# A chunked state-space scan feeding a maxout network: masks and exponents of the second chunk moved three groups forward, a weight decode moved into the next block, and the opening's transposes reordered

## The chip, the cores and the metric

The kernel runs on one core of one Trainium2 chip. The metric is the device time of one execution in microseconds (us); a smaller number is better. The instruction times below come from one profiled execution; the times of whole runs come from executions of the same program.

## The reference, cut to what matters

A Mamba2-like scan over 768 positions runs for 4 batches and 8 heads, with head size 32 and state size 16. Its output is laid out as 3072 tokens by 256 and goes through a maxout network with three input matrices and one output matrix.

```python
cum = np.cumsum(log_a_chunk, axis=-1)
L = np.exp(cum[:, :, :, None] - cum[:, :, None, :]) * causal
CB = np.einsum('bhin,bhjn->bhij', Cc, Bc)
y = einsum('bhij,bhjd->bhid', CB * L, xc) + einsum('bhin,bhnd->bhid', Cc, state) * exp(cum)
state = exp(sum la) * state + sum_j Bc[j] xc[j] * exp(cum[-1] - cum[j])
...
h = np.maximum(np.maximum(x @ w1, x @ w2), x @ w3)     # 256 -> 768
out = h @ w_out                                        # 768 -> 256
```

## The kernel before, in words

The sequence is cut into 6 chunks of 128 positions, numbered 0 to 5 (called c; the text counts chunk 1 as the second). For each chunk the attention part makes the 256-wide rows of 512 tokens (4 batches by 128 positions), called yT, and the network part of that chunk follows while the attention of the next chunk is worked on between its matmuls. The order on every engine is the order of the program text; nothing is rescheduled. TensorE (PE) makes all products into PSUM, VectorE (DVE) and ScalarE (ACT) empty PSUM, GpSimd (POOL) works between SBUF tiles, and almost all transfers are issued by SyncE (SP) in one order. Each transfer of SP uses one of eight completion semaphores in turn, and waits before it starts until the transfer eight places earlier on that semaphore has landed.

The stages around the change, in order:

- *Opening, chunk 0.* The decay matrix L0 of chunk 0 is made for the four batches b by matmuls into PSUM (`spread_i`, L335), an exponent straight from PSUM for b = 0 and 1 (`first_exps`, L367, ACT) or first a sum on DVE (`first_sums`, L362) for b = 2 and 3. B and C are transposed on PE (`scan_b`, `scan_tc`, both L434) and copied out by ACT (`BT` L430, `CT` L449, two instructions). `first_scores` (L533) multiplies them on PE, `first_weights` (L542, DVE) multiplies the scores into L0, four head pairs r = 0 to 3 for each pair of batches, and `first_own` (L607) makes y. Beside this, the running sums of the logarithms of all other chunks are made: `logs` (L267, ACT), `running` (L272, DVE, tile a_sb); SP writes them to DRAM (L962, rows_dram), reorders them (L966, cums), and later reads them back spread over the partitions, as L (`decay_load`, L390) and as E (`last_load`, L397, eight transfers).
- *Block 0.* A loop over n = 0 to 17 makes the maxout products of chunk 0 (`up`, L655, four 128x512 passes for each n) and evicts them (L1072 on ACT for the first matrix, L1074 on DVE for the maximum). The weights arrive in a packed form, so in every second n one piece is decoded: two ACT instructions (L184, L193), two on DVE (L185, L188), one on POOL (L194), which is `decode`, and one on DVE one round later (L197), which is `sign`. There are twelve pieces: nine for the three input matrices, and three for the output matrix.
- *Chunk 1's attention inside block 0.* `decay_masks` (L405, POOL, two instructions for each pair of batches) masks L, at n = 6 and n = 8. `part` makes one eighth of the exponents of L (L415, ACT, four instructions of 128x64), each after the mask of its pair. At n = 11 B and C are transposed. At n = 12 ACT makes the exponent of E (`scan_e`, L453), DVE makes Cd = C transposed times E (`scan_cd`, L460) and the scores go into four PSUM banks. `scan_weight` (L560, DVE) multiplies each bank of scores into L for one r: three of them stand on DVE's queue right behind Cd. At n = 14 `scan_state` (L504, tile A) needs two PSUM banks: the first is the bank that Cd reads and the second is the bank that the weighting of r = 0 reads. `scan_own` (L595) makes y from the weighted L; `scan_old` (L578) adds the part of the old state.
- *Block 1 and later.* The products of the network use a seven-product scheme for 2x2 blocks (`early` and `late`, both L705, for k = 0 to 8), with sums of yT (`scan_sums`, L630, DVE, four instructions of which each second one needs the one before it) and of weights (`weight_sums`, L690 to L693, POOL). In `early` the order of products is 1, 6, 5, 7; product 5 needs the first of the four yT sums, product 6 the second, product 7 the third. `early` is emptied by one ACT copy (L730) and three DVE sums (L731 to L733). Twelve pieces of chunk 0's output product (`down_next`, L891, four passes each) are put between them by a written list (X1, where each D is one piece): 1 and 2 pieces stand ahead of block 1, then one at k = 0, two at k = 1 and so on. The fifth and sixth piece need the last decoded part of the output matrix.

The parts of chunk 1's exponents and the downs of block 1 are placed by these lines:

```python
        if n in (6, 8):
            decay_masks(1, n - 6)
...
        part(1, {8: 1, 9: 2, 11: 1, 12: 2, 13: 1, 14: 1}.get(n, 0))
...
    X1 = ["tc", "DD", "D", "s", "D", "AD", "y", "D", "DD"]
```

Of the kernel before, what the change touches and what calls it, by code (L numbers as in the profile page):

```python
# [19 lines left out]
def kernel(  # L20
# [25 lines left out]
    NB, NH, S, D = x.shape  # L46
# [4 lines left out]
    NP = NH // 2  # L51
# [160 lines left out]
    def sign():  # L212

        unsigned.pop(0)()
# [50 lines left out]
    def logs(src, name):  # L265
        lg = const.tile(list(src.shape), FP32, name=name)
        nc.scalar.activation(lg, src, AF.Ln)  # L267
        return lg

    def running(rows, lg, out, keep):  # L270
        for w in range(out.shape[1]):
            nc.vector.tensor_tensor_scan(  # L272
                out=out[:, w], data0=keep[0:rows], data1=lg[:, w], initial=0.0,
                op0=ALU.mult, op1=ALU.add)
# [89 lines left out]
    def first_exps(b, summed, gs=range(2)):  # L364
        for g in gs:
            part = L0[:, b, g * HALF:(g + 1) * HALF]
            nc.scalar.activation(part, part if summed else spread[b, g], AF.Exp)  # L367
# [70 lines left out]
    def scan_tc(c, kind):  # L438
        st = blocks[c]
        st["trC"] = tr = kind([HN, NB, P], "trC")  # L440
        transposes(tr, st["C"])

    def scan_c(c):

        st = blocks[c]
        tr = st["trC"]
        st["CT"] = CT = att.tile([HN, NB, 2, P], FP32, tag="CT", bufs=1, name="CT")
        for g in range(2):
            nc.scalar.mul(CT[:, :, g], tr, parity[:, g:g + 1])  # L449
# [14 lines left out]
    def scan_bd(c):  # L464
        st = blocks[c]
        st["Bd"] = Bd = att.tile([P, BH, N], FP32, tag="Bd", bufs=1, name="Bd")
        nc.gpsimd.tensor_tensor(
            out=Bd, in0=st["B"], in1=from_j[c].unsqueeze(2).to_broadcast([P, BH, N]),
            op=ALU.mult)
# [233 lines left out]
    def products(c, k, which, first):  # L703
        for p, bank, half in which:
            nc.tensor.matmul(  # L705
                out=bank[:, half], lhsT=left(p, k), rhs=sides[c][p],
                start=(first and half == 0), stop=True, skip_group_check=True)
# [10 lines left out]
    def early(c, k):  # L718
        q, i = divmod(k, 3)
        A, B = (sum_bank(kind, [P, 2, HB]) for kind in "AB")  # L720
        products(c, k, [(1, A, 0), (6, A, 1), (5, B, 0), (7, B, 1)], True)
        if i == 0:
            held["m"] = ffn.tile([P, 4, HB], FP32, tag="m", name="m")

        if i > 0 and k % 2 not in quarters:
            quarters[k % 2] = kilos(HB)[:, 0:3]
        t = held["m"][:, 1:4] if i == 0 else quarters[k % 2]
        eu = wtmp.tile([P, 2, HB], FP32, tag="w_u", name="eu")
        v = wtmp.tile([P, 2, HB], FP32, tag="w_r", name="v")[:, 0]
        nc.scalar.copy(out=eu[:, 0], in_=A[:, 0])  # L730
        nc.vector.tensor_tensor(out=eu[:, 1], in0=A[:, 1], in1=eu[:, 0], op=ALU.add)  # L731
        nc.vector.tensor_tensor(out=v, in0=B[:, 1], in1=eu[:, 1], op=ALU.add)  # L732
        nc.vector.tensor_tensor(out=t[:, 2], in0=B[:, 0], in1=v, op=ALU.add)  # L733
        held["open"] = A, B, eu, t
# [215 lines left out]
    scan_b(0, ffn_bank)  # L950
    first_sums(2)
    scan_bd(0)
    first_exps(1, False)
    spread_banks(3, (att_bank, att_bank))
    spread_i((3,), True)
    clip(a_sb)
    first_sums(3)
    scan_tc(0, ffn_bank)
    scan_c(0)
    lg = logs(a_sb, "lg")  # L960
    running(R, lg, a_sb, keep2)
    nc.sync.dma_start(  # L962
        out=rows_dram.rearrange("k c s -> (k c) s").rearrange("(w r) s -> r w s", w=2), in_=a_sb)
# [17 lines left out]
    decode()  # L981
    first_exps(2, True, (1,))
    first_exps(3, True, (1,))
    s01 = first_scores(0)
    s23 = first_scores(2, {r: ffn_bank([P, 2, 2, P], "s") for r in (2, 3)})
    state_sum = first_state(att_bank)
    ncums_tp = turned(R, a_sb, "ncums", ffn_bank)
    first_weights(0, s01)

    aside = ffn.tile([P, 4, HB], FP32, tag="m", name="m")  # L990
    for j, s in enumerate(s23.values()):
# [59 lines left out]
    for n in range(NF * 3):  # L1051
        j, g = divmod(n, 2)
        q, i = divmod(j, 3)
        f = 2 * q + g
        if n == 0:
            pair = [ffn_bank([P, BLK], "up") for _ in range(2)]
            group(pair[0], 0, 0, (0,))
            first_own((2, 3))
            group(pair[1], 0, 1, (0,))
            for p, ff in zip(pair, range(2)):  # L1060
                group(p, 0, ff, (1,))
        if j > 0:
            p = ffn_bank([P, BLK], "up")
            whole_group(p, i, f)
        else:
            p = pair[g]
        if i == 0 and g == 0:
            m = ffn.tile([P, 4, HB], FP32, tag="m", name="m")
        pop({13: 2, 14: 1, 15: 2, 16: 1}.get(n, 0))
        mg = m[:, 2 * g:2 * g + 2].rearrange("p r t -> p (r t)")  # L1070
        if i == 0:
            nc.scalar.copy(out=mg, in_=p)  # L1072
        else:
            nc.vector.tensor_tensor(  # L1074
                out=mg if i == 1 else h_of(0)[:, f], in0=mg, in1=p, op=ALU.max)
        if g == 0 and n <= 16:
            sign()
            decode()
        if n == 1:
            fj = from_last(R, a_sb, "fj", HP)  # L1080
        if n == 3:
            first_tokens()
            load(2, "B")
            fetch()
            load(2, "C")
            fetch()
            decay_load(2, (0,))
            last_load(2)
            home(2, "x")
        if n in (6, 8):  # L1090
            decay_masks(1, n - 6)
        if n == 11:
            transposed(1)
            scan_bd(1)
            scan_c(1)
        if n == 12:
            scan_e(1)
            scan_cd(1)
            scores(1)
        part(1, {8: 1, 9: 2, 11: 1, 12: 2, 13: 1, 14: 1}.get(n, 0))  # L1100
        if n == 14:
            later.extend(scan_state(1, att_bank))
        if n == 15:
            shared["att"] = False
            places()
            weight_sums(0)
        if n == 16:
            scan_own(1, (0, 1))
        if n == 17:
            weight_sums(1)  # L1110
# [8 lines left out]
    pop(9)  # L1119
    transposed(2, False)  # L1120
    scan_bd(2)
    decode()
    down_next()
    down_next()

    X1 = ["tc", "DD", "D", "s", "D", "AD", "y", "D", "DD"]
    Y1 = 9 * [""]  # L1130
    P1 = [(1, 0, 0), (1, 0, 0), (0, 0, 2), (1, 0, 1), (0, 1, 1), (1, 1, 2), (1, 0, 1), (1, 0, 1),
          (1, 0, 2)]
# [10 lines left out]
    for c in range(1, NC):  # L1143
        n = c + 1
        xs, ys, ps_, ds, ks = (
            (X1, Y1, P1, D1, K1) if c == 1 else (X2, Y2, P2, D2, K2) if n < NC else
            (X3, Y3, P3, D2, {}))
        for k in range(NW):
            if k == 0 and n == NC:
                pop(1)  # L1150
            early(c, k)
            if c == 1 and k == 0:
                sign()
            part(n, ds[k][0])
            part(n + 1, ds[k][1])
            pop(ps_[k][0])
            if k == 0 and c > 1:
                if n < NC:
                    scan_bd(n)
                hidden_sums(c - 1, nc.gpsimd, (0 if c < NC - 1 else NQ - 1, NQ))  # L1160
            if c >= NC - 2 and k in (3, 6):
                hidden_sums(c, nc.gpsimd, (k // 3 - 1, k // 3))
            x = xs[k]
            if n == NC:
                last_next(k)
            elif x in ("D", "DD"):
                for _ in x:
                    down_next()
            elif x == "AD":
                later.extend(scan_state(n, att_bank))  # L1170
                down_next()
            elif x == "tc":
                scan_tc(n, att_bank)
                down_next()
            elif x == "t":
                transposed(n)
            elif x == "s":
                scores(n)
            elif x == "y":
                scan_old(n)  # L1180
                scan_own(n)
                scan_y(n)
                scan_sums(n)
            pop(ps_[k][1])
            maximum = late(c, k)
            if c == 1 and k + 2 < NW:
                weight_sums(k + 2)
            if c == 1 and k == NW - 2:
                output_weight_sums()
            if n < NC and k == 0:  # L1190
                loads(c + 2)
            if n < NC and k == 0:
                scan_c(n)
            if n < NC and k == int(c == 1):
                scan_e(n)
                later.append(lambda: scan_cd(n))
            flush()
            pop(ps_[k][2])
            later[:0] = maximum
            if ys[k] == "D":  # L1200
                down_next()
                flush()
            if k in ks and n + ks[k][0] < NC:
                decay_masks(n + ks[k][0], ks[k][1])
        if n == NC:
            pop(9)
        add_downs(c)
# [31 lines left out]
```

## Time and profile before

| what | value |
|---|---|
| median of three runs | 295.79 us (292.7 to 296.08) |
| the profiled execution's own time | 292.7 us |
| its span from first to last instruction | 291.0 us |
| PE busy | 278.3 us, 96% of the span |
| DVE, POOL, ACT busy | 209.3, 123.4, 111.9 us |
| DMA queue of the data | 88476 packets, 22.39 MB, 42.3% of 16 engines |

The profiled execution is the fastest of the three runs and lies 3.1 us under their median. A line of the timeline has the start and the duration in us, engine, line, operation, tiles, shape, count, and in brackets how long the engine was idle before it and what released it. SPq is SyncE issuing a transfer: its duration is that of the issue, not of the transfer. PE times of matmuls are pipelined, so a busy PE is not necessarily at its peak.

### The profile page before, as it was taken

How to read it: one execution, taken by the hardware profiler on the slowest of the kernel's cores; microseconds unless marked ns; L12 is line 12 of the kernel's file. 1: busy time of each engine (PE TensorE's matmuls, PEld its weight loads, DVE VectorE, ACT ScalarE, POOL GpSimd, SP SyncE). 2: the span in 40 equal slices, each digit the busy share in tenths (PEclk: the TensorE clock that was granted, in tenths of full speed). 3: DMA queues.
4: the chain of work that ended last, by engine and by line, in shares of the span. 5: the costliest groups of instructions: out<-in, count | busy, mean ns of one | idle time of the engine just before them, and what ended most of it. 6: DMA issues, size and time to landing. Idle time of an engine off the chain costs nothing.

```text
span 291.0 us, 7411 instructions
## 1 busy us (share of the span) xinstructions
PE 278.3 (96%) x3004; PEld 224.1 (77%) x3004; DVE 209.3 (72%) x414; ACT 111.9 (38%) x335; POOL 123.4 (42%) x143
## 2 busy tenths in 40 slices
PE   6899998999999999999999999999999999999995
PEld 4665443468877878888987888987888978988985
DVE  3586696858598697785867785867875876677682
ACT  2767467724454647223427223427212101111101
POOL 5173484398993974833004933004550403030300
PEclk9999999799999999999999999999999999999999
DMA  7969998979990008861006871001001001000103
GB/s 88 196 210 258 210 180 141 216 122 158 189 118 2 5 1 207 84 75 38 2 0 168 106 91 42 2 0 38 2 0 38 2 0 38 1 0 0 38 0 108
DMA packets 88957, 23.11 MB, mean 79 GB/s; under 512 B 80988, under 2 KB 84572, under 8 KB 88924
## 3 DMA queue, kind: packets, MB, share of 16 engines
q1 hardware_dynamic: 88476, 22.39, 42.3%
q8 instruction: 23, 0.38, 0.6%
q10 hardware_dynamic: 448, 0.26, 0.3%
q14 instruction: 10, 0.08, 0.1%
HBM read 19.40 MB, written 3.34 MB: 78 GB/s over the span
## 4 chain that ended last, share of the span: by engine, by line
PE 64%; DVE 12%; DMA 8%; SPq 6%; POOL 4%; ACT 2%; issue 2%; ACTq 0%; DVEq 0%; POOLq 0%
PE sumB L705 23%; PE sumA L705 16%; PE o L815 14%; SPq L134 3%; DMA raw_x<-in_x_dram 3%; DMA E<-cums 2%; DVE rb L630 2%; PE y L595 2%; PE s L552 2%; DMA rows_dram<-a_sb 2%; PE y L578 2%; PE o L891 2%; SPq L168 1%; DVE m L750 1%; PE spread L335 1%
## 5 line engine op out<-in xcount | busy, mean ns | idle before, releaser
L705 PE MATMUL sumA<-yT,w 128*128 128x256 f32 x180 | 54.9, 386 | 0.1
L790 POOL TENSOR_TENSOR hs<-h 128x256 f32<-128x256 f32 (+1 forms) x8 | 9.2, 1151 | 99.8 <-DVE h L750 99.8
L705 PE MATMUL sumB<-rb 128*128 128x256 f32 x180 | 46.2, 379 | 0.0
L730 ACT COPY eu<-sumA 128x256 f32<-128x256 f32 x45 | 16.8, 373 | 69.8 <-PE sumA L705 52.8
L415 ACT ACTIVATE L<-L,ncums 128x64 f32<-128x64 f32 x160 | 41.2, 340 | 2.8 <-POOL L L405 2.8
L705 PEld LDWEIGHTS sumB<-rb 128*128 128x128 f32 x180 | 34.2, 190 | 4.7
L705 PEld LDWEIGHTS sumA<-yT,w 128*128 128x128 f32 x180 | 30.4, 190 | 5.0 <-issue 0.7
L655 PE MATMUL up<-yT,w 128*128 128x512 f32 x64 | 30.8, 629 | 0.4 <-DVE w L197 0.4
L747 DVE TENSOR_TENSOR rb<-sumB,eu 128x512 f32<-128x512 f32 x30 | 20.8, 692 | 12.8 <-PE sumB L705 12.6
L705 PE MATMUL sumB<-yT,rb 128*128 128x256 f32 x90 | 28.0, 393 | 1.2 <-DVE m L733 0.6
L731 DVE TENSOR_TENSOR eu<-sumA,eu 128x256 f32<-128x256 f32 x45 | 18.9, 420 | 11.5 <-ACT eu L730 11.1
L194 POOL TENSOR_TENSOR w_u<-w_u,w_r 128x512 uint32<-128x512 uint32 x12 | 15.3, 1272 | 28.0 <-DVE w_u L188 21.6
L705 PE MATMUL sumA<-rb 128*128 128x256 f32 x90 | 26.8, 379 | 0.0
L705 PE MATMUL sumB<-rb,w 128*128 128x256 f32 x90 | 26.8, 379 | 0.0
L405 POOL TENSOR_SCALAR_AFFINE_SELECT L<-L 128x1024 f32<-128x1024 f32 (+1 forms) x20 | 24.2, 1208 | 0.7
L655 PEld LDWEIGHTS up<-yT,w 128*128 128x128 f32 x64 | 12.2, 199 | 15.0 <-issue 12.1
L732 DVE TENSOR_TENSOR v<-sumB,eu 128x256 f32<-128x256 f32 x45 | 19.1, 425 | 5.0 <-DVE eu L731 0.5
L705 PEld LDWEIGHTS sumB<-yT,rb 128*128 128x128 f32 x90 | 15.8, 189 | 7.5 <-DVE m L733 3.3
L705 PEld LDWEIGHTS sumA<-rb 128*128 128x128 f32 x90 | 17.1, 190 | 2.3
L705 PEld LDWEIGHTS sumB<-rb,w 128*128 128x128 f32 x90 | 17.1, 190 | 2.3
L815 PE MATMUL o<-wo,h 128*128 128x128 f32 x120 | 17.6, 280 | 0.6 <-DVE ob L824 0.6
L815 PEld LDWEIGHTS o<-wo,h 128*128 128x128 f32 x120 | 15.9, 191 | 2.8 <-ACT eu L730 1.1
(141 smaller groups left out, 496.1 us busy)
## 6 DMA issues: line engine op xcount, KB each, us to landing
L<-cums SPq DMA_DIRECT2D x20, 256.0 KB, 5.3
rb<-in_moe_w_dram SPq DMA_DIRECT2D x9, 512.0 KB, 6.2
raw_x<-in_x_dram SPq DMA_DIRECT2D x6, 512.0 KB, 7.5
out_dram<-ob SPq DMA_DIRECT2D x11, 256.0 KB, 2.1
raw_B<-in_B_dram SPq DMA_DIRECT2D x6, 256.0 KB, 4.8
raw_C<-in_C_dram SPq DMA_DIRECT2D x6, 256.0 KB, 6.7
rb<-in_moe_w_out_dram SPq DMA_DIRECT2D x3, 512.0 KB, 6.6
E<-cums SPq DMA_DIRECT2D x40, 32.0 KB, 3.9
```

Source lines behind the costliest of these rows:

```text
L134: nc.sync.dma_start(out=t, in_=src[:, :, c * P:(c + 1) * P, :].rearrange("b h s n -> s (b h) n"))
L194: nc.gpsimd.tensor_tensor(out=u, in0=u, in1=r, op=ALU.add)
L405: nc.gpsimd.affine_select(out=Ls[c][0:rows, b], in_=Ls[c][0:rows, b], pattern=[[0, 2], [0, NH], [1, HP]], compare_op=ALU.is_ge, fill=MASKE ...
L415: nc.scalar.activation(L[:, b, h], L[:, b, h], AF.Exp, bias=ncum[c][:, b * NH + h:b * NH + h + 1], scale=1.0)
L655: nc.tensor.matmul(out=bank, lhsT=w_sb[i][:, k, f * P:(f + 1) * P], rhs=yT[0][:, k], start=(k == 0), stop=(k == KD - 1))
L705: nc.tensor.matmul(out=bank[:, half], lhsT=left(p, k), rhs=sides[c][p], start=(first and half == 0), stop=True, skip_group_check=True)
L730: nc.scalar.copy(out=eu[:, 0], in_=A[:, 0])
L731: nc.vector.tensor_tensor(out=eu[:, 1], in0=A[:, 1], in1=eu[:, 0], op=ALU.add)
L732: nc.vector.tensor_tensor(out=v, in0=B[:, 1], in1=eu[:, 1], op=ALU.add)
L747: nc.vector.tensor_tensor(out=t[:, 0:2], in0=B, in1=eu[:, 1:2].to_broadcast([P, 2, HB]), op=ALU.add)
L790: eng.tensor_tensor(out=s1, in0=a21, in1=a22, op=ALU.add)
L815: nc.tensor.matmul(out=o[:, PLACES[p]], lhsT=token_sums[c][p][:, f, u], rhs=wo_of(p)[:, f], start=(p == first and f == 0), stop=True, skip ...
```

## The change: what it does

Three places are changed, all in the first 115 us.

1. In the opening, C's transposes (L434) and their two copies (L449) go ahead of the exponents of b = 1 and the last spread, and the weighting of head pair 0 of the first two batches (L542) goes ahead of the running sums (L272). On PE the scores themselves keep their place behind the last spread.
2. In block 0, the masks of chunk 1 go from n = 6 and 8 to n = 3 and 6, and the exponents from n = 8 to 14 to n = 5 to 13, one part each n from 7 on. Six of eight parts then stand ahead of E's exponent in ACT's order, where before there were four.
3. In block 1, the last `decode` goes behind the first `early`, its `sign` behind k = 1, one down piece ahead of block 1 and one at k = 1 go to k = 2 and k = 7, and the first `early` takes its products in the order 1, 5, 6, 7.

```diff
-        products(c, k, [(1, A, 0), (6, A, 1), (5, B, 0), (7, B, 1)], True)
+        products(c, k, [(1, A, 0), (5, B, 0), (6, A, 1), (7, B, 1)] if c == 1 and k == 0 else
+                 [(1, A, 0), (6, A, 1), (5, B, 0), (7, B, 1)], True)
...
     scan_bd(0)
+    scan_tc(0, ffn_bank)
+    scan_c(0)
     first_exps(1, False)
     spread_banks(3, (att_bank, att_bank))
     spread_i((3,), True)
     clip(a_sb)
     first_sums(3)
-    scan_tc(0, ffn_bank)
-    scan_c(0)
     lg = logs(a_sb, "lg")
+    s01 = first_scores(0)
+    first_weights(0, {0: s01[0]})
     running(R, lg, a_sb, keep2)
...
-    s01 = first_scores(0)
...
-    first_weights(0, s01)
+    first_weights(0, {r: s01[r] for r in range(1, NP)})
...
-        if n in (6, 8):
-            decay_masks(1, n - 6)
+        if n in (3, 6):
+            decay_masks(1, {3: 0, 6: 2}[n])
...
-        part(1, {8: 1, 9: 2, 11: 1, 12: 2, 13: 1, 14: 1}.get(n, 0))
+        part(1, {5: 1, 7: 1, 8: 1, 9: 1, 10: 1, 11: 1, 12: 1, 13: 1}.get(n, 0))
...
     scan_bd(2)
-    decode()
     down_next()
-    down_next()
-    X1 = ["tc", "DD", "D", "s", "D", "AD", "y", "D", "DD"]
+    X1 = ["tc", "D", "DD", "s", "D", "AD", "y", "DD", "DD"]
...
             if c == 1 and k == 0:
-                sign()
+                decode()
...
             flush()
+            if c == 1 and k == 1:
+                sign()
```

## The prediction

> **What bounds the kernel now.** I read the page first, then busy time by stretch, then the waits and the timeline of the first 115 us, because everything that moves lies there.
>
> ```profile
> PE 278.3 (96%) x3004; PEld 224.1 (77%) x3004; DVE 209.3 (72%) x414; ACT 111.9 (38%) x335; POOL 123.4 (42%) x143
> PE   6899998999999999999999999999999999999995
> PEclk9999999799999999999999999999999999999999
> ```
>
> PE is full in nearly every slice, so no engine other than PE can shorten the run except by removing a PE wait. The one slice with a clock of 7 is at 51 to 58 us. The next view gives two stretches around it (columns: PE, PEld, DVE, ACT, POOL busy, then PEclk).
>
> ```profile
> 48.75:52.16 3.41, 1.69 (x66) 0.81 (x64) 1.91 (x3) 3.10 (x11) 0.80 (x1) 1.00 1.04 108
> 52.16:55.57 3.41, 3.41 (x15) 1.46 (x5) 2.63 (x6) 3.41 (x12) 0.00 (x0) 0.50 1.28 214
> ```
>
> PE is busy for half of the first stretch and then runs at half clock for exactly one stretch. The timeline says why it was idle:
>
> ```profile
> 46.44 0.67 ACT L193 ACTIVATE w_r<-rb 128x512 f32<-128x512 uint32 x1
> ...
> 49.06 0.63 ACT L453 ACTIVATE E<-E 128x512 f32<-128x512 f32 x1 [1.96 <-issue]
> ...
> 49.73 0.69 DVE L460 TENSOR_TENSOR Cd<-trC,E 128x512 f32<-128x512 f32 x1 [1.58 <-ACT E L453]
> ...
> 50.52 0.27 PE L504 MATMUL A<-raw_x,Bd 64*32 64x64 f32 x2 [1.09 <-POOL w_u L194]
> 50.68 0.69 DVE L560 TENSOR_TENSOR L<-s,L 128x512 f32<-128x512 f32 x1 [0.26 <-ACT L L415]
> ...
> 51.42 0.84 PE L504 MATMUL A<-raw_x,Bd 64*32 64x64 f32 x62 [0.64 <-DVE L L560]
> ...
> 52.20 5.36 PE L655 MATMUL up<-yT,w 128*128 128x512 f32 x8
> ```
>
> ACT stands at E's exponent for 1.96 us; Cd, the first weighting and the two A banks follow, each within 0.1 us. (The POOL instruction named for A had ended at 49.56; A starts 0.1 us after Cd's end at 50.42, whose bank it takes.) PE loses 1.09 + 0.64 us, and eight `up` passes take 5.36 us where the same line's eight at 45.73 took 3.70: another 1.7 us. So this stall costs some 3.4 us, the largest of the run after the opening. ACT waits for the transfer of E. The trace's landing records (one for each of 16 DMA engines) have the eighth E transfer on 15 engines at 47.00 to 47.27 us and on the last one at 48.91. At 46.82 an instruction packet of 16 KB starts and takes 0.93 us:
>
> ```profile
> q8 instruction: 1, 0.02, 2.3%
> ```
>
> That is from the DMA view of 46.5 to 49 us. I read it as PE's own instruction stream (queue 8 has 23 such packets, 0.38 MB, near 6008 PE instructions at 256 to a packet, as the page below has it) delaying one engine's share of E. This reading is an inference from the coincidence.
>
> The opening, and one mask later on:
>
> ```profile
> 11.50 1.26 ACT L449 ACTIVATE CT<-trC,parity 128x512 f32<-128x512 f32 x2
> ...
> 12.82 2.01 PE L533 MATMUL s<-CT,BT 32*128 32x256 f32 x24 [1.35 <-ACT CT L449]
> 13.09 0.74 DVE L272 TENSOR_TENSOR_SCAN a_sb<-keep,lg 96x128 f32<-96x128 f32 x2 [0.83 <-ACT lg L267]
> 13.86 0.34 SPq L962 DMA_DIRECT2D rows_dram<-a_sb  x1
> 14.53 2.48 DVE L542 TENSOR_TENSOR L<-s,L 128x512 f32<-128x512 f32 x4
> 16.92 1.08 PE L607 MATMUL y<-L,raw_x 128*32 128x128 f32 x32
> 18.75 1.58 SPq L966 DMA_DIRECT2D cums<-rows_dram  x2
> ```
> ```profile
> 36.07 2.69 POOL L405 TENSOR_SCALAR_AFFINE_SELECT L<-L 128x1024 f32<-128x1024 f32 x2
> 37.68 1.36 DVE L185 TENSOR_SCALAR w_u<-w_u 128x512 f32<-128x512 f32 x1
> ```
>
> DVE's four weightings and two scans are one unbroken run up to y; SP waits for rows_dram until 18.73 us before it may read the sums back.
>
> **What the Trainium skill says.** "TensorE: Matmul & The Clock Gate" (Part 1, What's actually happening) has a half-rate clock decided in free-running windows of 3413 ns; here the half clock lasts 3.41 us after a window half idle. The busy windows fix no exact limit: 2.06 of 3.41 us busy at 11.20 to 14.61 did not slow it, 1.69 did. "Runtime: NRT & Kernel Launch" (Instruction fetch mechanics) says that a sequencer refills its instructions in 16 KiB blocks through its own DMA queue, which agrees with the 16 KB packets. "DMA: Bandwidth & Descriptors" (Why a DMA increments its semaphore by 16 and not by 1) says that only the full count of 16 means landed, which agrees with ACT starting 0.15 us after the last engine. "GPSIMD Engine Reference" (Specifications) says that POOL shares its SBUF interfaces with VectorE; L185 took 1.36 us beside the mask and 0.43 elsewhere.
>
> **The change part by part.**
>
> *Opening.* Nothing is added; four transposes, two copies and one weighting move. PE: C's transposes start at about 9.7 instead of 10.81 (C landed at 8.62 by the landing records), the last spread ends at 11.4 instead of 10.88. ACT: copies of C at 10.4 to 11.7, then exponents of b = 1 (2 x 0.6 us) to 12.7, so lg starts within 0.1 us of 12.65. The scores' first two banks are those of b = 1's spread, which these exponents free at 12.2 and 12.7: PE's scores start near 12.8 as now. The early copies gain nothing, since the wait passes from the copies to the exponents. DVE: the sums of b = 3 end at 12.8 instead of 12.27; the moved weighting waits for the fifth score matmul (13.9, as now), runs 0.68, and only then come the scans: 14.55 to 15.3 instead of 13.09 to 13.83. Behind the scans are queued two decode instructions (0.9 us) and three weightings (3 x 0.6), so these end near 17.8 instead of 17.0. Cost: y and `up` 0.8 us later on PE (0.5 to 1.0), and rows_dram issued 1.4 us later.
>
> Do the 1.4 us pass down SP's queue? The landing records say that rows_dram lies behind three earlier loads: on 15 engines it landed 0.3 us after the third weight load, 16.85 to 17.61, on the last at 18.73 (0.26 after). A transfer on idle queues takes 1.25 us from issue to first packet (cums: 18.75 to 20.0). Issued at 15.3 it is ready at 16.5, before the slow engine's turn near 18.2. So I take 0, with 0.4 likely at worst and 1.4 if the cover is gone.
>
> *Masks and exponents.* Two pairs of mask instructions (2.69 and 2.68 us on POOL) move from 36.07 and 40.89 to about 29.3 and 36.1; L has landed by 27.4 and 32.2. Beside them DVE loses time: at 36.07 and 40.89 L197 and L185 grew by (1.12 - 0.69) + (1.36 - 0.43) and (1.61 - 0.69) + (1.36 - 0.43), 1.4 and 1.9 us, and PE lost 0.36 and 0.34 us at 37.1 and 42.2 waiting for L197 (distance of matmul starts, less the usual 0.43). The new place at 29.3 hits the L197 that PE needs at 30.5: 0 to 0.9 us, less what PE is late by then; I take 0.3. The second place stays, the third place's loss goes. Sum on PE: about 0. On ACT one part (1.05 us) more stands at n = 5 and others at 7 to 10, in an idle stretch (4.34 us idle ahead of 32.59). Behind E only the parts for r = 2 and 3 of the second pair remain, so weightings r = 0 and 1 follow Cd at once: the 0.26 us wait goes, and the third comes at 51.8 instead of 53.07.
>
> So PE reaches the instructions at 46.8 about 0.5 us later (0.8 + 0.3 - 0.34 = 0.76, at least 0.4). Those instructions decide the fetch: it moves to 47.2 or later, when E's packets are done. E then lands at 47.3, not 48.9. ACT gets there at 47.6 (its queue follows PE), E's exponent ends at 48.3, Cd at 49.0, weighting 0 at 49.65; PE reaches A at 49.8 and waits for neither bank. It gains 51.42 - 49.8 = 1.6 us, and the half clock's 1.7 as no window is half idle: 3.3 us. The next limit is DVE and POOL: weighting 3, S and POOL's chain (old, S, weight sums, decode, 57.13 to 63.77 unbroken) come 1.7 to 2.0 us sooner, and that chain releases L197 and the yT sums (L630) that block 1 starts from. Of 3.3 us some 1.3 to 1.6 is lost there. Net: 1.7 us gained, between 1.0 and 2.6.
>
> *Block 1.* The decode's L185 and L188 (0.41 + 0.43 us) leave the place ahead of `early`'s DVE sums, so these come 0.7 us sooner; PE's wait there is 0.31 us and stays near 0.2. One down piece less (0.86 us) ahead of block 1 leaves less cover for L630, and order 1, 5, 6, 7 meets the sums as they come. POOL's decode goes from 68.69 to about 70 at today's clock, so weight sums of k = 2 end 1.3 us later, at 73.5; PE needs them near 75. The fifth down piece at k = 2 needs L197 at 74 to 75, within 0.5 us of its use. I take 0, -0.3 to +0.5. From there on all blocks are the same and PE-bound, so a gain or loss stays.
>
> **Sum.** On the profiled execution 292.7 - 1.7 = 291.0 us. The median of the runs lies 3.1 us above that execution for a reason I can't see; I take the same difference: 295.8 - 1.7 = 294.1 us.
>
> **Rivals.**
>
> *Same landing of E* (the fetch still meets it, or the 1.6 us is not the fetch): the A wait keeps its length but for 0.26 us, perhaps the half clock goes since PE comes later and idles less than 1.4 us; DVE's m, L197 and weighting 3 then allow about 0.7 us. Gain 0.2 to 0.9, time 295.4. For it: the fetch's cause is inferred. Against: PE is later by at least half the packet's time.
>
> *Slower: the opening's delay goes down the DMA chain.* If rows_dram lands more than 0.4 us later, its followers do too, because SP waits for each landing in turn until E; at the full 1.4 us E is ready at about 50.3, A's second bank at 52.4 instead of 51.42, and the half clock stays. Loss 1.0 (0.3 to 1.6), time 296.8. It decides from a landing of 19.2 us on. For it: DMA moves only 27 and 8 GB/s around 19 us, so nothing later fills in. Against: the backlog shown.
>
> *The early mask starves PE's weights:* at 0.9 us PE is late, but the A wait swallows it: 294.5.
>
> **How the numbers follow.** Forecast 0.48, same landing 0.29, slower 0.18, early mask 0.05. The range 291.5 to 296.9 us goes from the best end of the forecast (294.1 - 2.6 + 0 = 293.2 less 1.7 for the spread of runs before) to the slower rival. A measurement of this kernel tells 2% (5.9 us) from no change; no case reaches that, unless causes add up: faster 0.04, same 0.93, slower 0.03.
>
> **What would show it.** Right: ACT L453 starts by 48 us; no idle PE of 0.6 us at L504; PEclk full near 52; rows_dram landing near 18.8 though issued near 15.3; y at 17.8. Wrong: L453 at 49 or later, cums issued after 19.2, PE waits at L705's first sums over 0.6 us, or a span under 288.5 or over 292.5.

## The result, and the profile after

The changed kernel took 290.81 us (median of 36 runs, 289.15 to 295.5), the kernel before on the same chip 293.65 us (median of 45, 290.96 to 296.47). The ratio is 0.9938, with a 95% interval from 0.9919 to 0.9958: 1.8 us faster. That is less than 2%, but the interval does not reach 1. The ratio leaves out executions more than 1.5% above the fastest of their kernel, the medians hold them; that is why the medians are 2.84 us apart. The kernel before came out at 293.65 us here and not at the 295.79 of its first three runs, so the changed kernel's 290.81 us lies 3.3 us under the forecast 294.1, and 0.7 us under the lower end of its range, although the difference is the one that was forecast. The profiled execution took 291.13 us with a span of 289.4, against 292.7 and 291.0 before.

The page of the changed kernel, then its core view (span, mean granted clock) and the same two stretches as before (PE, PEld, DVE, ACT, POOL busy, PEclk). The granted clock is the share of TensorE's full clock that it was given: 1.00 is called full clock here, and 0.50 half clock.

```profile
PE 278.2 (96%) x3004; PEld 223.5 (77%) x3004; DVE 209.0 (72%) x414; ACT 112.1 (39%) x335; POOL 123.5 (43%) x143
PE   6889999989999999999999999999999999999995
```
```profile
core 0: 289.4 us, clock 1.000
```
```profile
48.75:52.16 3.41, 3.14 (x70) 1.51 (x69) 2.67 (x5) 3.33 (x11) 0.79 (x1) 1.00 1.23 217
52.16:55.57 3.41, 3.41 (x43) 1.41 (x41) 3.38 (x8) 0.83 (x2) 1.43 (x2) 1.00 1.10 204
```

PE has as much to do as before (278.2 against 278.3 us busy). The clock is full throughout this execution; in the stretch where PE was busy for 1.69 us it now is for 3.14. The timeline of that place:

```profile
48.83 0.63 ACT L453 ACTIVATE E<-E 128x512 f32<-128x512 f32 x1 [1.06 <-DMA E<-cums]
...
49.49 0.69 DVE L460 TENSOR_TENSOR Cd<-trC,E 128x512 f32<-128x512 f32 x1 [1.36 <-ACT E L453]
...
50.10 1.88 DVE L560 TENSOR_TENSOR L<-s,L 128x512 f32<-128x512 f32 x3
...
50.28 0.28 PE L504 MATMUL A<-raw_x,Bd 64*32 64x64 f32 x2
...
50.84 0.84 PE L504 MATMUL A<-raw_x,Bd 64*32 64x64 f32 x62 [0.27 <-DVE L L560]
...
51.61 3.70 PE L655 MATMUL up<-yT,w 128*128 128x512 f32 x8
```

ACT still waits for E: its exponent starts 0.23 us sooner, no more. What is new stands behind it: the three weightings (L560) follow Cd in one piece where the third used to come at 53.07, PE loses 0.27 us at the state products instead of 1.09 + 0.64, and the eight `up` passes take 3.70 us instead of 5.36. The opening:

```profile
12.26 2.49 PE L533 MATMUL s<-CT,BT 32*128 32x256 f32 x24 [0.81 <-ACT L L367]
...
13.60 0.69 DVE L542 TENSOR_TENSOR L<-s,L 128x512 f32<-128x512 f32 x1 [0.76 <-ACT w_u L184]
...
14.21 0.72 DVE L272 TENSOR_TENSOR_SCAN a_sb<-keep,lg 96x128 f32<-96x128 f32 x2
...
14.96 0.35 SPq L966 DMA_DIRECT2D rows_dram<-a_sb  x1
...
17.42 1.08 PE L607 MATMUL y<-L,raw_x 128*32 128x128 f32 x32
...
18.28 1.58 SPq L970 DMA_DIRECT2D cums<-rows_dram  x2
```

PE's wait passed from C's copies to the exponents, as forecast, and shrank from 1.35 to 0.81 us: the scores start 0.56 us sooner. y comes 0.5 us later all the same. rows_dram is issued 1.1 us later and cums 0.47 us sooner: the landing records have rows_dram at 16.80 to 17.20 us on 15 engines and 18.27 on the last.

Starts of the same PE instructions in traces (us; e2 and e9 are experiments below):

| | before | after | e2, masks and exponents alone | e9, E loaded sooner |
|---|---|---|---|---|
| first `up` (L647) | 18.70 | 19.21 | 18.79 | 18.12 |
| E's exponent (ACT) | 49.06 | 48.83 | 49.38 | 46.42 |
| state products L504, the piece that waits for the second bank | 51.42 | 50.84 | 51.39 | 48.78, no wait |
| last `up` of block 0 | 59.67 | 57.42 | 57.97 | 56.50 |
| span | 291.0 | 289.4 | 289.7 | 288.2 |

### The profile page after: what moved, and what is told of

It reads as the page before. It is cut to its first block, busy times and chain, and to the rows that moved or that the text cites. A ratio compares the mean times of both kernels' runs of the same rounds, so it can differ in the third digit from the quotient of the medians.

```text
span 289.4 us, 7412 instructions
## 1 busy us (share of the span) xinstructions
PE 278.2 (96%) x3004; PEld 223.5 (77%) x3004; DVE 209.0 (72%) x414; ACT 112.1 (39%) x335; POOL 123.5 (43%) x143
## 2 busy tenths in 40 slices
DMA packets 88957, 23.11 MB, mean 80 GB/s; under 512 B 80988, under 2 KB 84572, under 8 KB 88924
## 4 chain that ended last, share of the span: by engine, by line
PE 65%; DVE 13%; SPq 9%; DMA 4%; POOL 4%; issue 2%; ACT 2%; DVEq 0%; POOLq 0%; ACTq 0%
PE sumB L705 23%; PE sumA L705 16%; PE o L817 14%; SPq L134 4%; SPq L397 2%; DVE rb L630 2%; PE y L595 2%; PE o L893 2%; PE s L552 2%; DMA L<-cums 2%; PE y L578 2%; DVE L L560 1%; DVE m L752 1%; SPq L168 1%; SPq L390 1%
## 5 line engine op out<-in xcount | busy, mean ns | idle before, releaser
L705 PE MATMUL sumA<-yT,w 128*128 128x256 f32 x180 | 54.9, 386 | 0.1
L705 PE MATMUL sumB<-rb 128*128 128x256 f32 x180 | 46.5, 380 | 0.5 <-DVE rb L630 0.5
L705 PEld LDWEIGHTS sumB<-rb 128*128 128x128 f32 x180 | 34.0, 190 | 5.6 <-POOL rb L691 0.8
L705 PEld LDWEIGHTS sumA<-yT,w 128*128 128x128 f32 x180 | 30.5, 190 | 5.0 <-DVE h L748 0.7
L655 PE MATMUL up<-yT,w 128*128 128x512 f32 x64 | 29.6, 603 | 0.6 <-DVE w L197 0.4
L749 DVE TENSOR_TENSOR rb<-sumB,eu 128x512 f32<-128x512 f32 x30 | 20.8, 692 | 12.8 <-PE sumB L705 12.7
L705 PE MATMUL sumB<-yT,rb 128*128 128x256 f32 x90 | 28.0, 392 | 1.2 <-DVE m L735 0.8
L705 PE MATMUL sumA<-rb 128*128 128x256 f32 x90 | 26.8, 380 | 0.0
L705 PE MATMUL sumB<-rb,w 128*128 128x256 f32 x90 | 26.8, 379 | 0.0
L655 PEld LDWEIGHTS up<-yT,w 128*128 128x128 f32 x64 | 11.4, 189 | 14.6 <-issue 11.3
L705 PEld LDWEIGHTS sumB<-yT,rb 128*128 128x128 f32 x90 | 15.9, 189 | 7.4 <-DVE m L735 3.3
L705 PEld LDWEIGHTS sumA<-rb 128*128 128x128 f32 x90 | 17.0, 190 | 2.6 <-issue 0.3
L705 PEld LDWEIGHTS sumB<-rb,w 128*128 128x128 f32 x90 | 17.1, 190 | 2.3
```

The costliest lines, as they stand in the source:

```text
L655: nc.tensor.matmul(out=bank, lhsT=w_sb[i][:, k, f * P:(f + 1) * P], rhs=yT[0][:, k], start=(k == 0), stop=(k == KD - 1))
L705: nc.tensor.matmul(out=bank[:, half], lhsT=left(p, k), rhs=sides[c][p], start=(first and half == 0), stop=True, skip_group_check=True)
L749: nc.vector.tensor_tensor(out=t[:, 0:2], in0=B, in1=eu[:, 1:2].to_broadcast([P, 2, HB]), op=ALU.add)
```

## The experiments

Every kernel ran beside the kernel before on its chip. Ratios are to that kernel, with 95% intervals. The executions fall into groups by their mean granted clock, which are counted at the end. Each trace is of one execution; which group it fell into is said where it matters.

**The three parts alone.** e1 has only the opening's edits, e2 only masks and exponents, e3 only block 1's, e4 the change without the opening (some lines of each; the whole edits stand in the change's diff):

```diff
 # e1: transposes, copies and the weighting of head pair 0 moved
+    scan_tc(0, ffn_bank)
+    scan_c(0)
     first_exps(1, False)
...
+    s01 = first_scores(0)
+    first_weights(0, {0: s01[0]})
     running(R, lg, a_sb, keep2)
...
 # e2 (and e4)
+        if n in (3, 6):
+            decay_masks(1, {3: 0, 6: 2}[n])
...
+        part(1, {5: 1, 7: 1, 8: 1, 9: 1, 10: 1, 11: 1, 12: 1, 13: 1}.get(n, 0))
...
 # e3 (and e4)
-    X1 = ["tc", "DD", "D", "s", "D", "AD", "y", "D", "DD"]
+    X1 = ["tc", "D", "DD", "s", "D", "AD", "y", "DD", "DD"]
...
```

> The opening's part alone (C's transposes and copies sooner, one weighting ahead of the running sums). Theory A (the gain comes from the exponents that no longer stand behind E on ACT): no gain, ratio 0.999 to 1.004; PE about 0.5 us later at y, the wait at L504 as before or shorter by that 0.5 us, rows_dram issued 1 us later. Theory B (the gain comes from PE's instruction fetch meeting another transfer because PE is shifted by the opening): most of the gain here, ratio about 0.995, with L453 under 48.5 us and full clock near 52 us.

> The masks and exponents of chunk 1 alone. Theory A: most of the gain, ratio 0.992 to 0.996: the weighting of r = 0 within 0.1 us of Cd, the copy L1072 at n = 12 one us sooner, PE idle at L504 under 1.2 us (before 1.73), and full clock near 52 us. Theory B: little, ratio 0.998 to 1.0, L453 at 49 us and a half clock as before.

> The block 1 part alone (decode behind the first early, one down less ahead of it, products 1, 5, 6, 7). Both theories: within 0.3 us of before, ratio 0.999 to 1.001; the DVE sums of the first early 0.7 us sooner, PE's waits at L705 there not longer than 0.5 us in sum. A third theory, that this part is a good share of the gain: ratio 0.997 or less.

> The whole change without its opening part. Theory A: as good as the whole change or up to 0.3 us better, ratio 0.991 to 0.994. Theory B: at least 1 us of the gain is missing, ratio 0.997 or more.

Measured: e1 1.0021 (0.9986 to 1.0057), median 292.3; e2 0.9932 (0.9889 to 0.9975), 291.61; e3 0.9987 (0.9948 to 1.0026), 293.54; e4 0.9936 (0.9901 to 0.9972), 291.9; the kernel before 294.15. So masks and exponents hold the whole of the ratio, and block 1's edits nothing that can be measured. In the medians over all executions the opening counts too (292.3 against 294.15 for e1); why is taken up further on. The timeline of e2 shows what masks and exponents do:

```profile
49.38 0.63 ACT L453 ACTIVATE E<-E 128x512 f32<-128x512 f32 x1 [2.04 <-issue]
...
50.65 1.88 DVE L560 TENSOR_TENSOR L<-s,L 128x512 f32<-128x512 f32 x3
50.84 0.27 PE L504 MATMUL A<-raw_x,Bd 64*32 64x64 f32 x2 [0.93 <-issue]
...
51.39 0.84 PE L504 MATMUL A<-raw_x,Bd 64*32 64x64 f32 x62 [0.28 <-DVE L L560]
52.16 3.70 PE L655 MATMUL up<-yT,w 128*128 128x512 f32 x8
```

E is as late as ever here, even 0.3 us later than before, and PE gets past the state products no sooner than before. But it idles 1.21 us and not 1.73, and there is no half clock behind it. e1, in which the exponents stand as before, idles 1.23 + 0.64 us there and has the half clock (5.09 us for the eight passes). e5 (below) has the old exponents too, but idles only 0.59 + 0.64 us in its trace, and stays at full clock.

**Which half of e2.** e6 moves only the masks. e7 leaves the masks and spreads the exponents so that six parts stand ahead of E:

```diff
 # e6
-        if n in (6, 8):
-            decay_masks(1, n - 6)
+        if n in (3, 6):
+            decay_masks(1, {3: 0, 6: 2}[n])
 # e7
-        part(1, {8: 1, 9: 2, 11: 1, 12: 2, 13: 1, 14: 1}.get(n, 0))
+        part(1, {7: 1, 8: 1, 9: 1, 10: 1, 11: 2, 12: 1, 13: 1}.get(n, 0))
```

> Only the masks of the second chunk go from n = 6 and 8 to n = 3 and 6; the exponents stay at n = 8 to 14. Theory A1 (the gain is that six parts of the exponents stand ahead of E and only two behind it, so that the weightings and PE's state products follow Cd at once): little gain, ratio 0.998 to 1.001, the weighting of r = 2 still near 53 us and the half clock of 3.4 us near 52 stays. Theory A2 (the gain is POOL's mask pair leaving the place at 40.9 us, where it slows DVE's decode): ratio about 0.994, as with both.

> The masks stay at n = 6 and 8; the exponents of the second chunk go one part each to n = 7, 8, 9, 10, two to 11, one to 12 and 13, so that six parts stand ahead of E and two behind it, as in the change. Theory A1: most of the gain of 1.8 us comes back, ratio 0.994 to 0.997, weighting r = 0 starts within 0.1 us of Cd's end, no half clock near 52 us. Theory A2: ratio 0.999 to 1.001.

Measured: e6 0.9991 (0.9952 to 1.0031), e7 0.9996 (0.9967 to 1.0026). Neither half gains by itself. For e6 the ratio is that of A1, but its trace has no half clock, although the exponents stand as before:

```profile
47.78 0.63 ACT L453 ACTIVATE E<-E 128x512 f32<-128x512 f32 x1 [0.59 <-DMA E<-cums]
...
49.71 1.27 PE L504 MATMUL A<-raw_x,Bd 64*32 64x64 f32 x64
...
51.79 0.69 DVE L560 TENSOR_TENSOR L<-s,L 128x512 f32<-128x512 f32 x1 [0.75 <-ACT L L415]
...
53.82 1.95 PE L655 MATMUL up<-yT,w 128*128 128x512 f32 x4 [0.92 <-DVE w L197]
```

E had landed on all 16 engines by 47.63 us in this execution, with the instruction packet at 50.94: this is the chain that the prediction forecast for the change, and it came without the exponents being moved. What is left is A1's wait, 0.75 us at the third weighting and 0.92 us of PE at L197. For e7, A1 fell as I put it: not one of its 14 executions was free of half clock. Its timeline (of an execution that also had a long half clock in the opening, so that all times are later) has ACT standing at an exponent until the first mask is made, the second mask pair on POOL from 47.70 us, and PE waiting for weights that DVE makes slowly beside it:

```profile
43.78 1.06 ACT L415 ACTIVATE L<-L,ncums 128x64 f32<-128x64 f32 x4 [3.88 <-POOL L L405]
...
47.70 2.69 POOL L405 TENSOR_SCALAR_AFFINE_SELECT L<-L 128x1024 f32<-128x1024 f32 x2
47.78 1.60 DVE L197 SCALAR_TENSOR_TENSOR w<-rb,w_u 128x512 uint32<-128x512 uint32 x1 [0.26 <-POOL w_u L194]
...
49.44 3.15 PE L655 MATMUL up<-yT,w 128*128 128x512 f32 x4 [2.00 <-DVE w L197]
```

I read this as early masks being what lets the exponents go early.

**E's landing, the step that the forecast was built on.** e9 is the kernel before with E's eight transfers ahead of the weight load and x:

```diff
     load(1, "C")
+    last_load(1)
     fetch()
     load(1, "x")
-    last_load(1)
```

> The kernel before with one edit: the eight transfers of E (L397) are issued ahead of the weight load and of x of the second chunk instead of behind them, so E lands several us before it is needed, whatever meets it. Theory F (the prediction's: E's landing bounds the wait at the state products, and the change's gain would come from an earlier landing): L453 starts by 48 us behind its exponents, Cd follows, A (L504) starts near 49.7 with its second bank 0.3 us late at most, no half clock near 52, and about 1.5 us are gained; ratio 0.993 to 0.996, and no execution has a single half-clock stretch of 3.4 us. Theory A1 (the weightings' place behind the exponents bounds it): the weighting of r = 2 and the weight decode behind it (L197) stay late because four of eight exponent parts still stand behind E; PE waits about 1.1 us for L197 after A, and the ratio is 0.997 to 1.000.

Measured: 0.995 (0.9919 to 0.9981), median 291.31 against 293.31.

```profile
46.42 0.61 ACT L453 ACTIVATE E<-E 128x512 f32<-128x512 f32 x1
...
48.78 1.00 PE L504 MATMUL A<-raw_x,Bd 64*32 64x64 f32 x64
...
50.40 0.69 DVE L560 TENSOR_TENSOR L<-s,L 128x512 f32<-128x512 f32 x1 [0.74 <-ACT L L415]
...
52.44 1.95 PE L655 MATMUL up<-yT,w 128*128 128x512 f32 x4 [0.74 <-DVE w L197]
```

Both theories hold in part. With E in time nothing is lost at the state products, its trace has no half clock, and the gain is that of F; but two of its 22 executions had a mean clock near 0.994, where F allowed none. What A1 names is next: the weighting of r = 2 waits 0.74 us for its exponents, L197 behind it, and PE another 0.74. So E's landing and the exponents behind E are two cures for one stall.

**Both cures, and the opening taken apart.** e8 is the change without the weighting ahead of the running sums; e10 is e8 with E sooner.

```diff
 # e8 and e10, against the change
-    s01 = first_scores(0)
-    first_weights(0, {0: s01[0]})
     running(R, lg, a_sb, keep2)
...
     first_exps(3, True, (1,))
+    s01 = first_scores(0)
...
-    first_weights(0, {r: s01[r] for r in range(1, NP)})
+    first_weights(0, s01)
```

> The whole change but for one step: the weighting of head pair 0 stays behind the running sums, C's transposes and copies go sooner. By the prediction's steps y starts at 17.0 instead of 17.4 and the run gains 0.4 to 0.8 us against the change (ratio to the kernel before 0.991 to 0.993), as the weighting sooner gives PE nothing. If the weighting sooner is what holds the opening's clock or frees a bank that PE waits for, the time is that of the change or worse, and PE's wait ahead of the scores is again over 1.3 us.

> The change without the weighting ahead of the running sums, and with E's eight transfers ahead of the weight load and x. Theory F: another 0.5 to 1 us below the change, since E's exponent need not wait (1.06 us idle ahead of L453 in the change); ratio to before 0.988 to 0.992 and a median near 289.5. Theory A1: the exponents are already in time, so at most 0.3 us more: ratio 0.992 to 0.995, median 290.2 to 290.8. If the transfers of E delay the weight load behind them, PE waits at L197 near 38 to 42 us and it is slower.

Measured: e8 0.9951 (0.9921 to 0.9982), median 290.52 beside 293.46; e10 0.9927 (0.9891 to 0.9964), median 289.9 beside 293.31. e8's ratio missed what I expected of it: leaving the weighting in its place is worth nothing that can be told from the change. e10 has the lowest median of all kernels run, 3.4 us below the kernel before beside it; its ratio's interval overlaps that of the change, so that it beats the change is not shown. It lies between the two theories: the ratio is in A1's range, the median between the two. Its trace says what comes next: E is there in time and three weightings follow Cd in one piece, but x of the second chunk, now behind E, lands at 50.43 us, and PE waits 1.17 us for it at L504 (at 50.56).

**The long half clock in the opening.** The kernel before had executions near 296 us with a mean clock of 0.981 to 0.983. e4 has the opening of the kernel before, and its profile fell on an execution with that clock. Its opening by stretches of 3.41 us that start where the clock changed:

```profile
8.99:12.41 3.42, 2.06 (x33) 1.66 (x32) 2.41 (x6) 3.32 (x8) 0.00 (x0) 1.00 1.40 237
12.41:15.82 3.41, 1.21 (x16) 0.73 (x8) 3.38 (x8) 3.41 (x8) 2.28 (x2) 1.00 1.12 282
15.82:26.06 10.24, 9.47 (x111) 6.42 (x111) 4.20 (x8) 1.93 (x4) 3.16 (x3) 0.50 0.64 200
```

PE reached full clock at 5.58 us there, against 7.79 in the profile of before, so that the scores started 1.2 us sooner, at 11.61; x of the first chunk landed no sooner, and on the last engine 1.27 us later (15.75 against 14.48). PE then stood 2.27 us at L477, until 15.88. e7's profile is alike, and its timeline names x:

```profile
11.76 2.01 PE L533 MATMUL s<-CT,BT 32*128 32x256 f32 x24 [1.36 <-ACT CT L449]
15.61 0.79 PE L477 MATMUL A<-raw_x,Bd 128*32 128x64 f32 x32 [1.84 <-DMA raw_x<-in_x_dram]
```

In both, an instruction packet of 16 KB (at 13.02 and 12.84 us, 1.53 us long) comes before the last share of x, which lands on one engine at 15.75 and 15.47, over a microsecond after the other 15 (14.10 and 14.39). The packet alone does not do this: five other traces (e2, e6, e9, e10, e11) have such a packet at 12.83 to 13.01 us, and x on all 16 engines by 14.12 to 14.39. Why x is late only in the three traces with the earliest full clock (e4, e5, e7) stays open. Three experiments on this: e5 and e11 put matmuls into PE's wait ahead of the scores (their results are overwritten), five and two of them; e12 loads x ahead of the first weight piece, with the first decode behind the first weightings.

```diff
 # e5 (e11: range(2))
-    s01 = first_scores(0)
+    s01 = {r: att_bank([P, 2, 2, P], "s") for r in range(NP)}
+    for _ in range(5):
+        nc.tensor.matmul(
+            out=s01[0][:, 0].rearrange("j g i -> j (g i)"), lhsT=blocks[0]["BT"][:, 0],
+            rhs=blocks[0]["BT"][:, 0:2].rearrange("p b i -> p (b i)"), start=True, stop=True,
+            skip_group_check=True)
+    first_scores(0, s01)
 # e12
-    fetch()
     load(0, "x")
     fetch()
+    fetch()
...
-    decode()
     first_exps(2, True, (1,))
...
     first_weights(0, s01)
+    decode()
```

> The kernel before with five extra matmuls (128x256 each, about 0.21 us, written into the first score bank and overwritten by the real scores) in PE's wait ahead of the scores. Nothing else changes and their results are not used. Theory C (the opening part's worth is that PE idles less ahead of the scores, so that the clock gate does not take the half clock for 10.24 us from about 15.8 us on): PE's idle ahead of L533 falls from 1.35 to about 0.3 us, the scores start as before near 12.8, and no execution has the half clock in the opening; the median of all runs falls by 1.5 to 2 us, that of the undisturbed ones stays within 0.3 us. Theory D (the half clock there comes from elsewhere, for example from what the chip did before the launch): about four executions in ten still have it and the median stays at that of the kernel before.

> As the run with five extra matmuls ahead of the scores, but two (four passes, 0.85 us), so that they end before C's copies do. Theory C (PE's idle ahead of the scores, together with the one at L477, makes the half clock of 10.24 us): in executions that reach full clock near 5.7 us PE still waits 1 to 2 us at L477 for x, but the mean clock is not at 0.98 to 0.984 in more than one execution in ten; the median of all falls 1 to 2 us against the kernel before, that of the full-clock ones stays within 0.4 us. Theory D: about a third of the executions have that mean clock, as before.

> The kernel before with x of the first chunk loaded ahead of the first weight piece instead of behind it, and the first decode behind the first weightings so that ACT and DVE do not stand at it. Theory C2 (the half clock of 10.24 us in the opening comes from PE's wait at L477 for x, on top of the wait ahead of the scores, in executions whose clock windows lie so that PE reaches full clock near 5.7 us): x lands by 12.5 us, PE never waits at L477 for it, and no execution has a mean clock of 0.981 to 0.983, where about a third had it before; the median of all falls by 1 us or more, that of full-clock executions stays within 1 us (the weights land later: first up between 18.3 and 19.5). Theory D (it comes from elsewhere): about a third keep that clock.

Measured: e5 1.0111 (1.0054 to 1.0167), e11 1.0032 (1.0 to 1.0063), e12 1.0054 (1.003 to 1.0079): none is a better kernel. Of e5's six executions none had a mean clock near 0.98 (17 of 51 had it before in that job, so none of six would come by chance about once in eleven), and its profile is of the kind that reaches full clock early (5.75 us), waits at L477 (1.10 us), and stays at full clock, with the extra work in the window:

```profile
12.58:15.99 3.41, 2.31 (x53) 1.81 (x56) 3.27 (x7) 3.04 (x6) 2.03 (x2) 1.00 1.12 296
```

With two matmuls (e11), 7 of 22 still had it: Theory C as I wrote it, with PE's idle ahead of the scores as the cause, fell. That leaves the idle of the whole window, the wait for x included, as the likely cause; it is not shown. e12 speaks for x: none of 16. But the kernel before had it in only 3 of 21 in that job, and e12 paid with late weights (PE waits 2.80 us for L197 at 20.83, and each of its 16 executions had half clock somewhere, in the trace 3.41 us from 22.12 on). e5's median is not explained by its opening: some 1.4 us went between 181 and 183 us, where PE waited 1.28 us at L705. An instruction packet at 180.09 us stands beside it, but the kernel before has one at 179.97 and no such wait. I did not test that.

**How often each kernel had half clock.** Executions by mean granted clock, to within 0.002; in the traces, 0.994 goes with one stretch of 3.41 us (before, e1), 0.988 with 6.83 (e3, e8), 0.982 with 10.24 (e4). The mean does not tell where in the run the stretch lies. (Of the change one more execution is on record with its clock than the median holds.)

| kernel | executions | 0.997 or more | 0.994 | 0.988 | 0.983 or less |
|---|---|---|---|---|---|
| before, in the four jobs | 180 | 58 | 43 | 22 | 57 |
| e1, opening alone | 14 | 9 | 4 | 1 | 0 |
| e2 and e4, masks and exponents, old opening | 38 | 22 | 0 | 3 | 13 |
| e8 and e10, with C's transposes sooner | 33 | 28 | 2 | 3 | 0 |
| e9, E sooner, old opening | 22 | 12 | 2 | 0 | 8 |
| the change | 37 | 32 | 3 | 1 | 1 |

The single stretch is rare where masks and exponents are moved (5 of 108 in e2, e4, e8, e10 and the change, 43 of 180 before); for e9, 2 of 22 are too few to tell. The long one is rare wherever C's transposes and copies are sooner (1 of 84). At full clock alone most medians differ by less than 1 us: 291.23, 290.80 and 291.38 us for before in the first three jobs, 290.39 for e2, 290.91 for e4, 290.34 for e8, 290.87 for e9, 290.58 for the change; only e10, at 289.89, is 1.5 us below the kernel before beside it. By these counts more than half of the gain is that executions with half clock become rarer. The profile before is of one with a single stretch, as about one in four was, and the profile after of one without.

## Why the prediction was right in its difference, and where it was wrong

The forecast was 1.7 us faster (294.1 from 295.79); the ratio says 1.8, the two profiles 1.6. Of its signs, no idle PE of 0.6 us at L504 and full clock near 52 us came true, L453 by 48 us did not. The lower end of its range is 294.1 - 2.6 = 291.5 us; the 293.2 that it names on the way is 295.8 - 2.6. By its steps:

- **Opening, right in kind.** The wait passed to the exponents of b = 1; y and `up` are 0.5 us later where 0.8 was taken. The scores started at 12.26 and not near 12.8. rows_dram's later issue cost nothing: it landed 0.46 us sooner on the last engine. The slower rival decided from a landing at 19.2 us on, and it was 18.27.
- **Masks, nearly right.** PE's stalls are 0.27, 0.37 and 0.40 us at 30.8, 34.6 and 38.5, against 0.36 and 0.34 before: about 0.3 more, where about 0 was taken. The mask at 29.73 stretched L185 to 1.36 us, as the row of before had it.
- **"E then lands at 47.3, not 48.9": this step failed.** The packet did move, from 46.82 to 52.01, past E. That is 5.2 us, where PE reached its instructions there only 0.9 us later, so PE's delay is not what sets its place as I had it; e2 and e6, with the opening of the kernel before, have it at 46.84 and 50.94. Yet E landed at 48.35 to 48.68 on all 16 engines. The whole chain of loads was late, the eighth E transfer issued 1.53 us later and landing 1.35 us later, with single late shares among L's transfers (28.2 to 33.8). What made these late is open: another packet at 23.07 stands ahead of them, but e8 and e11 have one at 23.54 and 23.11 and L by 31.8, e3 and e10 have one near 21 and L only at 34.1 or later. I moved the packet and held the rest of the chain still. L453 started at 48.83, not by 48. "ACT gets there at 47.6" and "waits for neither bank" fell with it.
- **The gain at A was mis-sized.** Of 1.6 us only 0.58 came (50.84 against 51.42). The half clock was worth 1.66 us in the eight `up` passes, as taken (1.7). Of the sum of 2.25 us at the last `up`, 0.7 was lost until the end (1.3 to 1.6 of 3.3 was taken). A gain 1.0 us too large and a loss 0.6 to 0.9 us too large nearly cancelled: that the difference came out so close is luck in part.
- **The packet and the late share of E are more than one coincidence.** Five traces have a packet at 46.6 to 47.3 us. In four of them (before, e1, e2, e5) the last share of E lands 0.85 to 2.04 us after the other 15; in e11 it does not. In the nine traces without one there the last share is at most 0.05 us behind. How the packet does it is not shown.
- **The rival "same landing of E" had the mechanism and not the size.** It said that the half clock perhaps goes if PE idles less than 1.4 us; e2 idles 1.21 and shows just that, as do e5 (1.23) and e10 (1.17); before and e1, with 1.73 and 1.87, have the half clock. It gave 0.2 to 0.9 us, since DVE's L197 was to hold PE. That bound holds where the third weighting waits for its exponents (e9: 0.74 us at L197); with two parts behind E it doesn't, and L197 at 53.04 in e2 stops nobody.
- **Block 1, right.** Less cover for L630 was forecast, and PE waits for it at product 5 (0.45 us at 63.70); e3 measured 0.9987.
- **What I did not see.** The median's distance from the profiled execution, "for a reason I can't see", was by the counts the long half clock of the opening: 57 of 180 executions before had a mean clock of 0.983 or less, and their median is 295.9 us, as two of the first three runs were. That it lies in the opening was traced in e4 and e7, which have the old opening, not in the kernel before itself. The early copies, which I costed at no gain, take it away; the profile that I read was of an execution without it.

The Trainium skill, "TensorE: Matmul & The Clock Gate" (Part 1, What's actually happening), has the window free-running and so the warm-up different from run to run. The traces agree: 13 profiled kernels reach full clock at 5.58 to 8.61 us, a spread of 3.0 us, less than one window (the trace of the change holds no change of clock). I had cited that section for the length of the window and not asked what another position of it does to the opening.

What stays open is why C's earlier copies suffice. In e8's profile, at full clock from 6.3 us, PE idles 0.80 us ahead of the scores and 0.98 at L477, and there is a half clock of 6.83 us; yet its span is 290.0. No trace of the change or of e1 fell on an execution with full clock near 5.7 us.

## What to carry to other kernels

Where a half-idle stretch is followed by half clock, look both for work that can be taken out of the queue behind a late transfer and for a way to make the transfer earlier: e2 and e9 gained about the same, and in e2 0.5 us of idle less was worth 1.7 us in the executions that had the half clock. A transfer put ahead makes another one later, as x in e10. Look at the mean clock of every execution, not at one profile: if executions of one kernel fall into groups, find a trace of each group, because a change may act on the group that the profile doesn't show. And when a small transfer or packet is moved in an argument, move all that shares its queues too.

## What was not expected of the hardware

- Half clock came in stretches of one, two and three windows: 3.41, 6.83 and 10.24 us. Windows with PE busy for 0.63 (e3), 1.21 (e4), 1.42 and 1.57 (e7), 1.56 (e1) and 1.69 us (before) were followed by it, windows with 2.06 (before), 2.20 (e2) and 2.31 us (e5) were not. One with 2.43 us (e8, 13.13 to 16.54) was, so busy time as the profile has it is not the whole measure. At half clock, windows with 2.60 to 2.72 us (e3, e4, e7, e8) were followed by another at half clock, and in the last one before full clock PE was busy throughout (3.41 us in all eight stretches); but e4 and e7 also have a first one with 3.35 and 3.42 us that was followed by half clock.
- The executions with the earliest full clock were the slower ones in the traces (e4, e7): PE at double pace from 5.6 or 5.8 us on reached the wait for x sooner, x's last share landed about a microsecond later, and half clock followed.
- Where a 16 KB instruction packet ran as E landed, one engine's share was 0.85 to 2.04 us behind the other 15 in four of five traces. For x it was so in three of eight (15.75 against 14.10 us in e4), so a packet beside a load does not always delay it. PE started 0.13 us after the last share in e4, not after the 15.
